# Decay attention and two MLPs in one kernel: seven instead of eight inner blocks of the first MLP beside attention, and three smaller moves

## The chip, the cores and the metric

The kernel runs on one core of one Trainium2 chip. The metric is the device time of one execution in microseconds (us). Three runs of the kernel before gave 1080.03, 1080.71 and 1081.43 us; their median, 1080.71 us, is the time before.

## The reference

Attention over 4 batches of 8 heads with 576 positions and 64 columns per head, with a decay from a cumulated logarithm and a causal mask; then a leaky MLP over all 2304 tokens; then a gated MLP.

```python
B, H, S, D = 4, 8, 576, 64
scores = np.matmul(q, k.transpose(0, 1, 3, 2)) / np.sqrt(D)
cum = np.cumsum(np.log(np.clip(f, 0.0001, 1.0)), axis=-1)
scores = np.where(causal, -1e9, scores + cum[:, :, :, None] - cum[:, :, None, :])
attn = softmax(scores)                      # max taken off, 1e-9 added to the sum
x = (attn @ v).transpose(0, 2, 1, 3).reshape(2304, 512)
h = x @ w_in                                # 512 -> 2048
x = (np.maximum(h, 0) + alpha * np.minimum(h, 0)) @ w_out
out = ((x @ w_a) * (x @ w_b)) @ w_out2      # 512 -> 1536 -> 512
```

The weights come in double precision. Products are made in parts: a number is split into a first, rounded part and a rest, and three matmuls (first by first, first by rest, rest by first) stand for one.

## The kernel before

**Attention with a part of the first MLP.** 32 heads go one after the other through the list in `order(u)`: scores (tiles `sc`), softmax (`softmax_in`), two halves of the probabilities in fp16 (`p_hi`, `p_lo`), a DMA transpose, and the product with v (`pv`, two heads later). The v of a head is scaled and split into two fp16 parts by `split_v`, three operations on GpSimd (POOL) for 26 of the 32 heads. The first MLP's 16 inner blocks of 128 columns are cut into three groups: blocks 0 to `F1A`-1 are made beside attention, blocks to 11 in a first pass over all tokens afterwards, blocks 12 to 15 in a second pass (`PASSES`). What stands beside attention is `mlp1a`: for each half batch of 288 tokens, 12 matmuls for each block's hidden part (tiles `h`) and 12 for its share of the output (tiles `y`), so 24 matmuls of 288 columns for each block and half batch. A batch's MLP can begin once its 8 heads are done; `rates` says how much of it stands beside each head. `before_x` makes the program finish batch 0 before batch 2 takes its buffers.

**Weights.** Each weight block goes through `rounded` and `parts`: a DMA on SyncE's queue, an Abs on ScalarE (ACT, L138), three integer operations on VectorE (DVE, L140 to L142), a copy on ACT (L146) and a subtraction on POOL (L147). Beside attention there is one staging buffer; the list `ws` names the head at which each of the 16 weights (8 `in`, then 8 `out`) is issued.

**The two passes** go over the tokens in blocks of 384: 24 matmuls of 384 columns for each inner block (tiles `hb` and `ya`). The second pass ends with `pair_parts`: the second MLP is made with seven products in place of eight for a pair of token blocks, and wants sums and differences of the pair's quarters. `put` splits one such quarter sum (ACT copy L942, POOL subtraction L943) and writes it to DRAM through one of four `yhl` buffers.

**The second MLP** visits the three pairs of token blocks in three groups of inner blocks: 36 slots of seven products (tiles `p`, 6 matmuls of 384 columns each, from weights `w_a` and `w_h`), whose sums are multiplied in `both` into tiles `gg`, and then into the output (tiles `o`) one slot later or more, in `unit`. Weights `b` take four DVE subtractions and five tiles' worth of parts (tile `w_h`); `when` says at which slot the later weights are issued.

A scheduler with its own timeline reorders the instructions of each engine; every engine then executes its own row in order. So the order on an engine, not the code alone, says what stands behind what.

Of the kernel before, what the change touches and what calls it, by code (L numbers as in the profile page):

```python
# [13 lines left out]
AF = mybir.ActivationFunctionType  # L14
ALU = mybir.AluOpType
# [3 lines left out]
B, H, S, D = 4, 8, 576, 64  # L19
T = B * S  # L20
# [11 lines left out]
TB = 384  # L32
# [13 lines left out]
    psm=3,  # L46
    first=10,
    rates=[0, 1, 1, 1, 0.8, 1.15, 1.15, 0.95],
    ws=[0, 1, 2, 3, 4, 5, 6, 7, 8, 8, 9, 9, 10, 10, 11, 11],
    native=10,  # L50
    pre=1,
    we=0,
# [14 lines left out]


LAGM = 2
F1A = _P.get("f1a", 8)  # L70

F1B = 12
PASSES = (F1A, F1B), (F1B, NF1)
# [9 lines left out]
FG = 4  # L83
# [9 lines left out]
def decay_attention_then_two_mlps(ctx, tc, q, k, v, f, w_in, w_out, alpha, w_a, w_b, w_o, out):  # L93
    nc = tc.nc
    pe, dve, act, pool, sp = nc.tensor, nc.vector, nc.scalar, nc.gpsimd, nc.sync

    left, mid, right = ExitStack(), ExitStack(), ExitStack()
    def lpool(stack, name, bufs, side="left", **kw):
        return stack.enter_context(tc.tile_pool(name=name, bufs=bufs, side=side, reuse_waits="tile", **kw))
# [49 lines left out]
    def weight(kind, i, p, after=None):  # L149

        x = rounded(kind, i, after)
        if kind == "b":

            xa = ap_["xa"]
            s = mp["stage"].tile([128, 8, 128], F32, tag="ws", name=f"ws_{i}", bufs=1)
            t = W["h", i] = p.tile([128, 2, 10, 128], F32R, tag="h", name=f"w_h{i}")
            dve.tensor_tensor(s[:, 0:2], x[:, 0:2], xa[:, 0:2], op=ALU.subtract)
            dve.tensor_tensor(s[:, 2:4], x[:, 2:4], s[:, 0:2], op=ALU.subtract)
            dve.tensor_tensor(s[:, 4:6], x[:, 2:4], x[:, 0:2], op=ALU.subtract)
            dve.tensor_tensor(s[:, 6:8], xa[:, 2:4], s[:, 2:4], op=ALU.subtract)  # L160
# [163 lines left out]
    def split_v(n):  # L324

        if whole(n):
            return
        vs = ap_["vs", n % 3]
        t = halves(n)
        scale = ap_["vm", (n // H) % 2][:, 1:2]  # L330
        pool.tensor_scalar(vs[:, :, 2], vs[:, :, 1], scale, 1.0, op0=ALU.mult, op1=ALU.mult)
        pool.tensor_scalar(t[:, :, 0:D], vs[:, :, 2], 1.0, 0.0, op0=ALU.mult, op1=ALU.add)
        pool.tensor_tensor(t[:, :, D:], vs[:, :, 2], t[:, :, 0:D], op=ALU.subtract)

    def halves(n):
# [456 lines left out]
    if True:  # L792
        w1 = lpool(left, "w1", 2 * F1A)
# [103 lines left out]
        yp = lpool(pctx, "passes", 4)  # L897
        todo = [(kind, i, w1) for i in range(F1B, NF1) for kind in ("in", "out")]
        todo += [(kind, i, hp[0] if kind == "b" else w1) for i in range(2) for kind in "abo"]
        todo += [("o", 2, w1), ("a", 2, w1)]  # L900
        bl = list(blocks())
        runs = [(p, t0, n) for p in range(2) for t0, n in bl]
        due = 0.0
# [27 lines left out]
                    continue  # L931
                pair_parts(t0 // TB, e, ya)

        kept = {}

        def pair_parts(blk, e, ya):

            pair, odd = divmod(blk, 2)

            def put(x, j, c):  # L940
                yh = yp.tile([128, 2, TB], F32R, tag="yhl", name=f"yhl_{pair}_{j}_{c}")
                act.copy(yh[:, 0], x)  # L942
                pool.tensor_tensor(yh[:, 1], x, f32(yh[:, 0]), op=ALU.subtract)  # L943
                sp.dma_start(f32(yq_d)[:, pair, j, c::2], f32(yh))

            if not odd:
                kept[e] = ya[e]
                put(ya[e], 0 if e < 2 else 3, e % 2)
            elif e >= 2:
                c = e - 2  # L950
                a11, a12, a21, a22 = kept[c], kept[e], ya[c], ya[e]
                s1 = yp.tile([128, TB], F32, tag="s1", name=f"s1_{pair}_{c}", bufs=2)
                dve.tensor_tensor(s1, a21, a22, op=ALU.add)
                put(s1, 2, c)
                dve.tensor_tensor(a21, a11, a21, op=ALU.subtract)
                put(a21, 5, c)
                dve.tensor_tensor(a11, s1, a11, op=ALU.subtract)
                put(a11, 1, c)
                put(a22, 6, c)
                dve.tensor_tensor(a12, a12, a11, op=ALU.subtract)  # L960
                put(a12, 4, c)

        Y = []
        visits = [0, 1, 2, 1, 0, 1, 2]
# [12 lines left out]
        for ri, (p, t0, n) in enumerate(runs):  # L977
            f0, f1 = PASSES[p]
            xh, xl = cur
            if ri + 1 < len(runs):  # L980
                cur = load_pair(xh_d, xl_d, *runs[ri + 1][1:], f"x{runs[ri + 1][0]}")
            st = {}
            for fi in range(f0, f1):
                w = W["in", fi]
                hps = pst.tile([128, 512], F32, tag="mm", name=f"hb_{t0}_{fi}")
                for c in range(C):
                    mm3(hps[:, :n], w[:, 0, c], w[:, 1, c], xh[:, c, :n], xl[:, c, :n], c == 0, c == C - 1)
                g = gp_.tile([128, 2, TB], F32R, tag="g", name=f"gb_{t0}_{fi}")
                leaky(hps, n, fi, tp, g[:, 0, :n], g[:, 1, :n])
                later(partial(passes_out, p, t0, n, fi, g, st))  # L990
                due += 0.4
                while len(todo) > 0 and due >= 1 and (ri, fi) > (0, f0 + 1):
                    due -= 1
                    weight(*todo.pop(0), ap_["last"])
                if p and t0 == 0 and fi == f0 + LAGM - 1:
                    w2ctx.close()
                    mp["yq"] = lpool(right, "yq", 4, "right")
                    ga_ = lpool(right, "ga", 3, "right")
                if p and t0 in (3 * TB, 5 * TB) and fi == f0:
                    for _ in range(4 if t0 == 3 * TB else 2):  # L1000
                        load_y()
        load_y()
        while todo:
            weight(*todo.pop(0), ap_["last"])
        while behind:
            behind.pop(0)()
        load_y()
        pctx.close()
        hp.append(lpool(left, "h2", FG // 2))
        op_ = lpool(left, "os", 3)  # L1010


        turns = [(g_, pair) for g_ in range(NG) for pair in range(NPAIR)[::(1, -1)[g_ % 2]]]
        slots = [(i, fi) for i in range(len(turns)) for fi in range(FG)]
        when = {0: [("b", 2), ("a", 3)], 1: [("b", 3), ("o", 3)]}
        for g_ in range(1, NG):
            s_ = (g_ * NPAIR - 1) * FG
            for fi in range(FG):
# [125 lines left out]
```

## Time and profile before

| what | value |
| --- | --- |
| median of three runs | 1080.71 us |
| profiled execution, its own time | 1082.8 us |
| its span, first to last instruction | 1081.0 us |
| TensorE busy (matmul) | 1011.7 us, 94% |
| VectorE busy | 717.5 us, 66% |
| ScalarE busy | 502.9 us, 47% |
| GpSimd busy | 560.4 us, 52% |
| granted clock of TensorE, mean | 0.976 |

Times in rows are us from the span's start. A matmul's duration overlaps that of the next, so the distance from one start to the next is what it costs in a dense row. PE is TensorE, PEld its weight loads. The shares are means over stages with different limits; what a change is worth is read stage by stage.

### The profile page before, as it was taken

To read this page: it belongs to the slowest core of one execution; us is meant where nothing else is said; L and a number is where in the kernel's file an instruction comes from. 1 tells how busy PE (TensorE), PEld (TensorE's weight loads), DVE (VectorE), ACT (ScalarE), POOL (GpSimd) and SP (SyncE) were. 2 spreads that over 40 slices of the span, in tenths; PEclk is the share of its full clock that TensorE was granted. 3 is DMA by queue.
4 is the path that set the end of the run, shared out by engine and by line. 5 is a ranking of instruction groups with operands and counts; after the bars stand their busy time and mean duration, and the time that the engine had idled before them with its cause. 6 is when DMAs were issued, how large, how long until landed. Compare 5 with 4: busy or idle time off the path is not lost.

```text
span 1081.0 us, 18236 instructions
## 1 busy us (share of the span) xinstructions
PE 1011.7 (94%) x6207; PEld 942.6 (87%) x6207; DVE 717.5 (66%) x1504; ACT 502.9 (47%) x1222; POOL 560.4 (52%) x662
## 2 busy tenths in 40 slices
PE   5989766999999999999999996899999999999998
PEld 3667655999899999999999995899989999899997
DVE  6688899558878836253457666655986558974553
ACT  6878866668778744333343533322433113321110
POOL 4366998747879845343346857522444224541111
PEclk9989977999999999999999998899999999999999
DMA  5776967757697495476767997636327383454623
GB/s 147 182 179 194 197 142 146 157 163 138 124 206 149 91 276 173 157 236 234 233 230 260 354 377 254 241 116 253 107 88 271 138 306 123 130 189 159 243 88 108
DMA packets 235969, 204.24 MB, mean 189 GB/s; under 512 B 152228, under 2 KB 209060, under 8 KB 235876
## 3 DMA queue, kind: packets, MB, share of 16 engines
q1 hardware_dynamic: 231268, 198.36, 62.0%
q10 hardware_dynamic: 4608, 4.72, 1.3%
q8 instruction: 49, 0.80, 0.3%
q14 instruction: 44, 0.36, 0.1%
HBM read 131.55 MB, written 50.17 MB: 168 GB/s over the span
## 4 chain that ended last, share of the span: by engine, by line
PE 55%; DVE 8%; POOL 4%; issue 3%; ACT 2%; DMA 1%; POOLq 0%; DVEq 0%; ACTq 0%
PE p L736 7%; PE p L738 7%; PE p L737 7%; PE o L738 4%; PE o L737 4%; PE o L736 4%; PE ya L737 3%; PE hb L738 3%; PE hb L736 3%; PE hb L737 3%; PE ya L738 3%; PE ya L736 3%; PE y L737 1%; PE y L738 1%; PE y L736 1%
## 5 line engine op out<-in xcount | busy, mean ns | idle before, releaser
L736 PE MATMUL p<-yq,w_h 128*128 128x384 f32 x360 | 122.6, 341 | 7.9 <-ACT w_h L146 6.4
L737 PE MATMUL p<-yq,w_h 128*128 128x384 f32 x360 | 122.0, 339 | 0.0
L738 PE MATMUL p<-yq,w_h 128*128 128x384 f32 x360 | 121.4, 338 | 0.0
L1077 POOL TENSOR_TENSOR gg<-tc,gg 128x384 fp32r<-128x384 f32 x36 | 37.0, 1027 | 113.5 <-ACT gg L1076 103.2
L736 PE MATMUL o<-w_o,gg 128*128 128x512 f32 x216 | 84.8, 394 | 4.1 <-ACT gg L1076 4.1
L1077 POOL TENSOR_TENSOR gg<-td,gg 128x384 fp32r<-128x384 f32 x36 | 37.3, 1036 | 93.7 <-ACT gg L1076 87.9
L737 PE MATMUL o<-w_o,gg 128*128 128x512 f32 x216 | 85.1, 394 | 0.0
L738 PE MATMUL o<-w_o,gg 128*128 128x512 f32 x216 | 84.4, 395 | 0.0
L736 PE MATMUL y<-g,w_out 128*128 128x288 f32 x256 | 78.0, 310 | 6.1 <-ACT w_out L146 4.2
L733 POOL TENSOR_TENSOR gb<-lt,gb 128x384 fp32r<-128x384 f32 x48 | 50.0, 1042 | 62.5 <-ACT gb L732 62.5
L736 PE MATMUL h<-xh,w_in 128*128 128x288 f32 x256 | 77.4, 305 | 3.7 <-DVE lt L731 3.4
L736 PEld LDWEIGHTS p<-yq,w_h 128*128 128x128 f32 x360 | 68.1, 189 | 12.4 <-ACT w_h L146 6.9
L737 PE MATMUL y<-g,w_out 128*128 128x288 f32 x256 | 76.9, 303 | 1.9 <-POOL g L733 1.9
L428 ACT ACTIVATE s<-s,nm 128x512 f32<-128x512 f32 (+3 forms) x128 | 71.4, 559 | 11.2 <-DVE nm L427 10.5
L1076 ACT CAST gg<-tc 128x384 fp32r<-128x384 f32 x36 | 18.5, 514 | 123.4 <-DVE tc L1075 122.9
L737 PE MATMUL h<-xl,w_in 128*128 128x288 f32 x256 | 75.7, 296 | 0.0
L738 PE MATMUL h<-xh,w_in 128*128 128x288 f32 x256 | 75.2, 294 | 0.0
L731 DVE SCALAR_TENSOR_TENSOR lt<-lu,nal,hb 128x384 f32<-128x384 f32 x48 | 29.3, 611 | 68.3 <-ACT lu L730 66.7
L738 PE MATMUL y<-g,w_out 128*128 128x288 f32 x256 | 74.2, 300 | 0.1
L737 PEld LDWEIGHTS p<-yq,w_h 128*128 128x128 f32 x360 | 68.1, 189 | 3.5
L427 DVE CUSTOM_DVE_ANT_0 s<-sc,maskz 128x512 f32<-128x512 f32 (+3 forms) x128 | 60.2, 485 | 12.9 <-PE sc L415 6.9
L738 PEld LDWEIGHTS p<-yq,w_h 128*128 128x128 f32 x360 | 67.8, 188 | 0.2
(217 smaller groups left out, 3307.2 us busy)
## 6 DMA issues: line engine op xcount, KB each, us to landing
yq<-yq_d SPq DMA_DIRECT2D x49, 768.0 KB
yq_d<-yhl SPq DMA_DIRECT2D x42, 384.0 KB
yl<-ya_d SPq DMA_DIRECT2D x48, 192.0 KB
po_d<-os SPq DMA_DIRECT2D x36, 256.0 KB
os<-po_d SPq DMA_DIRECT2D x36, 256.0 KB
wr_in<-in_moe_w_in SPq DMA_DIRECT2D x16, 512.0 KB
wr_out<-in_moe_w_out SPq DMA_DIRECT2D x16, 512.0 KB
wr_a<-in_moe_w_a SPq DMA_DIRECT2D x12, 512.0 KB
```

The source lines that it names most:

```text
L427: dve.tensor_tensor_reduce(s, o, m, -0.125, 3.0e38, ALU.add, ALU.min, nm)
L428: act.activation(s, s, AF.Exp, bias=nm, scale=-1.0, accum_out=sm)
L731: dve.scalar_tensor_tensor(t, u, nal[:, fi:fi + 1], hp[:, :n], op0=ALU.mult, op1=ALU.add)
L733: pool.tensor_tensor(gl, t, f32(gh), op=ALU.subtract)
L736: pe.matmul(o, lh, rh, start=start, stop=False)
L737: pe.matmul(o, lh, rl, start=False, stop=False)
L738: pe.matmul(o, ll, rh, start=False, stop=stop)
L1076: ap_["last"] = act.copy(g[:, 0], o).ins
L1077: pool.tensor_tensor(g[:, 1], o, f32(g[:, 0]), op=ALU.subtract)
```

## The change

Four edits. `F1A` is 7 and not 8: one block fewer beside attention for each half batch, one more (block 7) in the first pass, two of the `w1` weight buffers moved to the first pass's pool, and a list `ws` of 14 weights. In `split_v` the first fp16 part is made on ACT from the loaded v, with the scale, and no longer on POOL from the scaled v. The third `b` weight of the second MLP is issued during the passes into a pool of its own, and not at the second MLP's slot 0. And for the last pair of token blocks the sums of `pair_parts` are put off: ten steps, of which one is issued after each of the first ten products of the second MLP.

```diff
-    ws=[0, 1, 2, 3, 4, 5, 6, 7, 8, 8, 9, 9, 10, 10, 11, 11],
+    ws=[0, 1, 2, 3, 4, 5, 6, 7, 7, 8, 8, 9, 9, 10],
-F1A = _P.get("f1a", 8)
+F1A = _P.get("f1a", 7)
         pool.tensor_scalar(vs[:, :, 2], vs[:, :, 1], scale, 1.0, op0=ALU.mult, op1=ALU.mult)
-        pool.tensor_scalar(t[:, :, 0:D], vs[:, :, 2], 1.0, 0.0, op0=ALU.mult, op1=ALU.add)
+        act.activation(t[:, :, 0:D], vs[:, :, 1], AF.Copy, scale=scale)
         pool.tensor_tensor(t[:, :, D:], vs[:, :, 2], t[:, :, 0:D], op=ALU.subtract)
...
-        todo += [("o", 2, w1), ("a", 2, w1)]
+        todo += [("o", 2, w1), ("a", 2, w1), ("b", 2, hp)]
...
+            def less(o, x, y, j, c):
+                dve.tensor_tensor(o, x, y, op=ALU.subtract)
+                put(o, j, c)
...
-                put(s1, 2, c)
-                dve.tensor_tensor(a21, a11, a21, op=ALU.subtract)
-                put(a21, 5, c)
-                dve.tensor_tensor(a11, s1, a11, op=ALU.subtract)
-                put(a11, 1, c)
-                put(a22, 6, c)
-                dve.tensor_tensor(a12, a12, a11, op=ALU.subtract)
-                put(a12, 4, c)
+                steps = [
+                    partial(put, s1, 2, c),
+                    partial(put, a22, 6, c),
+                    partial(less, a21, a11, a21, 5, c),
+                    partial(less, a11, s1, a11, 1, c),
+                    partial(less, a12, a12, a11, 4, c),
+                ]
+                if blk == T // TB - 1:
+                    put_off.extend(steps)
+                    return
+                for step in steps:
+                    step()
...
                     ga_ = lpool(right, "ga", 3, "right")
+                    hp.append(lpool(right, "h2", FG // 2, "right"))
...
-        while todo:
-            weight(*todo.pop(0), ap_["last"])
+        assert not todo
...
-        when = {0: [("b", 2), ("a", 3)], 1: [("b", 3), ("o", 3)]}
+        when = {0: [("a", 3)], 1: [("b", 3), ("o", 3)]}
...
                 if leaves:
                     load_y()
+                if put_off:
+                    put_off.pop(0)()
                 return o
```

What the scheduler makes of it is seen in the order of the engines. First TensorE at heads 16 and 17. `sc_16` and `sc_17` are scores of these heads, `y_0_0` the output of batch 0's first half batch, `w_out7` and `w_out6` the last weight that it needs before and now, `tqk_17` a transpose for head 17. Before:

```order
L414 MATMUL sc_17_3_2570<-U1_1_156,T1_1_155 128x512
L415 MATMUL sc_17_3_2570<-TU2_1_157 128x512
L414 MATMUL sc_17_1_2597<-U1_1_156,T1_1_155 128x256
L415 MATMUL sc_17_1_2597<-TU2_1_157 128x256
L738 MATMUL y_0_0_0_1611<-g_0_0_1233,w_out7_1593 128x288
L738 MATMUL y_0_0_1_1697<-g_0_0_1233,w_out7_1593 128x288
L738 MATMUL y_0_0_2_1768<-g_0_0_1233,w_out7_1593 128x288
L414 MATMUL sc_17_0_2605<-U1_1_156,T1_1_155 128x128
L415 MATMUL sc_17_0_2605<-TU2_1_157 128x128
```

Now:

```order
L738 MATMUL y_0_0_0_1572<-g_0_0_1243,w_out6_1383 128x288
L738 MATMUL y_0_0_1_1655<-g_0_0_1243,w_out6_1383 128x288
L738 MATMUL y_0_0_2_1723<-g_0_0_1243,w_out6_1383 128x288
L380 MATMUL tqk_17_0_2263<-ident_90,qkn_17_2114 128x96 x3
L380 MATMUL tqk_17_1_2273<-ident_90,qkn_17_2114 128x96 x3
L414 MATMUL sc_16_2_2291<-U1_0_147,T1_0_146 128x384
L414 MATMUL sc_16_0_2312<-U1_0_147,T1_0_146 128x128
L415 MATMUL sc_16_2_2291<-TU2_0_148 128x384
L415 MATMUL sc_16_0_2312<-TU2_0_148 128x128
```

The last matmuls of `y_0_0` stood among head 17's scores and now stand ahead of head 16's; the rest of batch 0 follows them directly in both orders. Counted over the whole order, the `h` and `y` matmuls in TensorE's row are, before and now: ahead of head 16's first score 150 and 147, from head 16's first score to head 18's 240 and 195, from there to head 31's 630 and 552, and behind it 516 and 450; in all 1536 and 1344.

Second, GpSimd where the first MLP ends and the second begins. `yhl_2_*` are the last pair's parts (`put`), `gg_s_b` the products of slot s (block b of the pair), `w_h2` and `w_h3` the third and fourth `b` weight. Before:

```order
L1077 TENSOR_TENSOR gg_1_0_8342<-tc_1_8281,gg_1_0_8342 128x384
L943 TENSOR_TENSOR yhl_2_5_0_8128<-yl_1_1920_0_8072,yhl_2_5_0_8128 128x384
L943 TENSOR_TENSOR yhl_2_1_0_8133<-yl_1_1536_0_7908,yhl_2_1_0_8133 128x384
L943 TENSOR_TENSOR yhl_2_6_0_8137<-yl_1_1920_2_8090,yhl_2_6_0_8137 128x384
L1077 TENSOR_TENSOR gg_1_1_8385<-td_1_8282,gg_1_1_8385 128x384
L943 TENSOR_TENSOR yhl_2_4_0_8142<-yl_1_1536_2_7944,yhl_2_4_0_8142 128x384
L943 TENSOR_TENSOR yhl_2_2_1_8149<-s1_2_1_8147,yhl_2_2_1_8149 128x384
L943 TENSOR_TENSOR yhl_2_5_1_8154<-yl_1_1920_1_8074,yhl_2_5_1_8154 128x384
L943 TENSOR_TENSOR yhl_2_1_1_8159<-yl_1_1536_1_7910,yhl_2_1_1_8159 128x384
L943 TENSOR_TENSOR yhl_2_6_1_8163<-yl_1_1920_3_8092,yhl_2_6_1_8163 128x384
L943 TENSOR_TENSOR yhl_2_4_1_8168<-yl_1_1536_3_7946,yhl_2_4_1_8168 128x384
L147 TENSOR_TENSOR w_h2_8225<-wx_b2_8219,w_h2_8225 128x256
```

Now:

```order
L1087 TENSOR_TENSOR gg_0_1_8200<-td_0_8097,gg_0_1_8200 128x384
L943 TENSOR_TENSOR yhl_2_2_0_8105<-s1_2_0_8087,yhl_2_2_0_8105 128x384
L943 TENSOR_TENSOR yhl_2_6_0_8117<-yl_1_1920_2_8056,yhl_2_6_0_8117 128x384
L943 TENSOR_TENSOR yhl_2_5_0_8130<-yl_1_1920_0_8038,yhl_2_5_0_8130 128x384
L943 TENSOR_TENSOR yhl_2_1_0_8143<-yl_1_1536_0_7874,yhl_2_1_0_8143 128x384
L943 TENSOR_TENSOR yhl_2_4_0_8166<-yl_1_1536_2_7910,yhl_2_4_0_8166 128x384
L147 TENSOR_TENSOR w_h3_8263<-wx_b3_8257,w_h3_8263 128x256
L943 TENSOR_TENSOR yhl_2_2_1_8182<-s1_2_1_8090,yhl_2_2_1_8182 128x384
L943 TENSOR_TENSOR yhl_2_6_1_8195<-yl_1_1920_3_8058,yhl_2_6_1_8195 128x384
L1087 TENSOR_TENSOR gg_1_0_8282<-tc_1_8206,gg_1_0_8282 128x384
L147 TENSOR_TENSOR w_h3_8263<-ws_3_8262,w_h3_8263 128x512
L943 TENSOR_TENSOR yhl_2_5_1_8216<-yl_1_1920_1_8040,yhl_2_5_1_8216 128x384
```

The third `b` weight stood behind all ten of the last pair's parts and is now far ahead of them, in the passes; seven parts now stand between slot 0's second product and slot 1's first, where three of them stood between slot 1's two products before.

## Rows read from the trace of the kernel before

**Rows 1.** Windows: length; busy us (count) of PE, PEld, DVE, ACT, POOL; PE clock; DMA.
```profile
101.80:173.20 71.40, 52.76 (x385) 45.33 (x383) 66.27 (x171) 55.53 (x154) 64.75 (x81) 0.88 0.79 175
173.20:190.90 17.70, 11.18 (x61) 9.11 (x60) 14.22 (x37) 10.01 (x29) 12.68 (x18) 0.69 0.78 142
190.90:225.90 35.00, 35.00 (x264) 34.35 (x263) 14.78 (x32) 18.24 (x48) 20.19 (x29) 0.96 0.73 190
225.90:365.70 139.80, 136.70 (x1153) 130.76 (x1152) 113.88 (x318) 112.93 (x324) 110.83 (x168) 1.00 0.68 142
365.70:442.90 77.20, 75.36 (x593) 73.94 (x593) 39.48 (x73) 37.23 (x90) 42.14 (x46) 1.00 0.64 184
442.90:664.00 221.10, 220.78 (x1261) 219.67 (x1260) 127.41 (x201) 87.78 (x177) 117.62 (x106) 1.00 0.79 269
664.00:682.00 18.00, 7.53 (x22) 5.95 (x21) 7.97 (x11) 6.55 (x15) 13.13 (x13) 0.62 0.56 201
```

**Rows 2.** Timeline of GpSimd, the last two `w_out` weights beside attention.
```profile
173.67 1.76 POOL L147 TENSOR_TENSOR w_out<-wx_out,w_out 128x512 fp32r<-128x512 f32 x1 [0.45 <-ACT w_out L146]
...
188.78 1.28 POOL L147 TENSOR_TENSOR w_out<-wx_out,w_out 128x512 fp32r<-128x512 f32 x1
```

**Rows 3.** Timeline of TensorE, batch 0's outputs around 190 us.
```profile
188.44 0.61 PE L736 MATMUL y<-g,w_out 128*128 128x288 f32 x1 [1.85 <-ACT w_out L146]
...
189.08 0.44 PE L736 MATMUL y<-g,w_out 128*128 128x288 f32 x1
189.32 0.44 PE L737 MATMUL y<-g,w_out 128*128 128x288 f32 x1
...
194.27 0.29 PE L738 MATMUL y<-g,w_out 128*128 128x288 f32 x1
194.40 0.29 PE L736 MATMUL y<-g,w_out 128*128 128x288 f32 x1
```

**Rows 4.** Groups by line and shape, GpSimd and VectorE, 101.8 to 173.2 us.
```profile
L332 POOL TENSOR_SCALAR vs<-vs 128x320 f16<-128x320 f32 x6 | 3.7, 623 | 0.2
...
L142 DVE SCALAR_TENSOR_TENSOR wx_out<-wr_out,wx_out 128x512 int32<-128x512 int32 x7 | 6.7, 956 | 0.1
```

**Rows 5.** The same groups, ScalarE and GpSimd, 225.9 to 365.7 us.
```profile
L486 ACT ACTIVATE p_hi<-s,ri 128x384 f16<-128x384 f32 x13 | 8.0, 614 | 1.6 <-DVE ri L451 1.1 <-issue 0.2
...
L622 ACT ACTIVATE x<-pv,vm 64x256 f32<-64x256 f32 x13 | 6.1, 469 | 0.7 <-PE pv L597 0.3
...
L332 POOL TENSOR_SCALAR vs<-vs 128x320 f16<-128x320 f32 x12 | 5.5, 459 | 0.5
```

**Rows 6.** Timeline of VectorE and of GpSimd, 660 to 665 us.
```profile
660.38 1.37 DVE L955 TENSOR_TENSOR yl<-yl,yl 128x384 f32<-128x384 f32 x1
...
664.36 0.54 DVE L955 TENSOR_TENSOR yl<-yl,yl 128x384 f32<-128x384 f32 x1
...
660.19 1.14 POOL L943 TENSOR_TENSOR yhl<-s,yhl 128x384 fp32r<-128x384 f32 x1 [1.65 <-ACT yhl L942]
```

**Rows 7.** Timeline of TensorE where the second MLP begins.
```profile
668.84 0.80 PE L736 MATMUL o<-w_o,gg 128*128 128x512 f32 x1 [4.09 <-ACT gg L1076]
...
677.10 0.69 PE L736 MATMUL p<-yq,w_h 128*128 128x384 f32 x1 [6.38 <-ACT w_h L146]
...
678.55 0.52 PE L736 MATMUL p<-yq,w_a 128*128 128x384 f32 x1
678.87 0.52 PE L737 MATMUL p<-yq,w_a 128*128 128x384 f32 x1
...
685.00 0.41 PE L736 MATMUL p<-yq,w_h 128*128 128x384 f32 x1 [1.24 <-DVE td L1093]
...
685.60 0.33 PE L736 MATMUL p<-yq,w_h 128*128 128x384 f32 x1
685.77 0.34 PE L737 MATMUL p<-yq,w_h 128*128 128x384 f32 x1
```

**Rows 8.** Timeline of ScalarE at the same place.
```profile
673.41 0.51 ACT L942 CAST yhl<-yl 128x384 fp32r<-128x384 f32 x1 [2.97 <-DMA yq_d<-yhl]
```

More of the change, by code (lines that the diff above doesn't have):

```diff
@@ L932, in passes_out @@
                 pair_parts(t0 // TB, e, ya)
-        kept = {}
+        kept, put_off = {}, []
         def pair_parts(blk, e, ya):
@@ L993, in decay_attention_then_two_mlps @@
                     due -= 1
-                    weight(*todo.pop(0), ap_["last"])
+                    kind, i, pl = todo.pop(0)
+                    weight(kind, i, pl[1] if pl is hp else pl, ap_["last"])
                 if p and t0 == 0 and fi == f0 + LAGM - 1:
@@ L1002, in decay_attention_then_two_mlps @@
         load_y()
-        while todo:
-            weight(*todo.pop(0), ap_["last"])
+        assert not todo
         while behind:
@@ L1007, in decay_attention_then_two_mlps @@
         load_y()
-        pctx.close()
-        hp.append(lpool(left, "h2", FG // 2))
-        op_ = lpool(left, "os", 3)
         turns = [(g_, pair) for g_ in range(NG) for pair in range(NPAIR)[::(1, -1)[g_ % 2]]]
         slots = [(i, fi) for i in range(len(turns)) for fi in range(FG)]
-        when = {0: [("b", 2), ("a", 3)], 1: [("b", 3), ("o", 3)]}
+        when = {0: [("a", 3)], 1: [("b", 3), ("o", 3)]}
         for g_ in range(1, NG):
@@ L1061, in decay_attention_then_two_mlps @@
         for s_, (i, fi) in enumerate(slots):
+            if s_ == FG - 2:
+                assert not put_off
+                pctx.close()
+                op_ = lpool(left, "os", 3)
             g_, pair = turns[i]
```

## The prediction

> **What bounds the kernel now.** I read the windows view by stage first, then the counts in the engines' orders, then timelines at the places where a stage's busiest engine stands still. Stage bounds are the starts of heads' first score matmuls, counted off in TensorE's timeline (head 10 at 101.8 us, 16 at 173.2, 17 at 190.9, 18 at 225.9, 31 at 365.7); batch 3's MLP ends at 442.9, the passes at 664.
>
> [Rows 1] show four different limits. Heads 10 to 15: TensorE is busy 52.8 of 71.4 us, VectorE 66.3 (93%) and GpSimd 64.8 (91%); the two small engines bind, at a granted clock of 0.88. Head 16, 17.7 us: nothing is full, TensorE 11.2 at clock 0.69. What it waits for is batch 0's first output, which needs every `w_out` weight: the last two are split at 173.7 and 188.8 [rows 2], and TensorE's `y` rows wait for them [rows 3]. From 190.9 to 225.9 TensorE is full (35.0 of 35.0): batch 0 must be finished before later heads may go on. Heads 18 to 30: TensorE 136.7 of 139.8 (98%), VectorE, ScalarE and GpSimd 79 to 81%; TensorE binds. Up to 664 it stays full. At 664 to 682 it works 7.5 of 18 us, at clock 0.62, and [rows 7] name the three stalls: 4.09 us for a `gg`, 6.38 us for `w_h` and 1.24 us for a sum.
>
> **The change part by part.** Prices are against the profiled execution, 1082.8 us, 2.1 above the median of the three runs; I take 2.1 off at the end.
>
> *One inner block moves.* In a dense row a 288-column matmul costs 0.13 us (194.27 to 194.40 in [rows 3]), a 384-column one 0.173 (685.60 to 685.77 in [rows 7]). Removed beside attention: 24 matmuls x 8 half batches = 192. Added to the first pass: 24 x 6 token blocks = 144, and the passes are full of matmuls (220.8 of 221.1 us, [rows 1]), so they cost all of 144 x 0.173 = **+24.9 us**. For TensorE alone that is an exchange (192 x 0.13 = 25.0); what counts is how much of the 25 us the attention stages give back, and how much idle time goes with it.
>
> - Head 31 and batch 3: 66 fewer matmuls (516 to 450 in the order) where TensorE is busy 75.4 of 77.2 us: 66 x 0.13 = **-8.6**. Two weights more (10, not 8) are made here; VectorE, ScalarE and GpSimd are at 48 to 55%, which hides them. If that cover failed the passes would wait for one staging chain.
> - Heads 18 to 30: 78 fewer matmuls, 78 x 0.13 = 10.1 us if TensorE goes on binding, nothing if another engine takes over. ScalarE's 112.9 us get 13 more activations of 320 columns (between 0.469 for 256 and 0.614 for 384, [rows 5], so about 0.54 each, +7.0) and lose some three leaky blocks, about 2.5; 117 us in 130 would be 90%. VectorE's 113.9 less 2 in 130 is 86%. VectorE has been 93% full in heads 10 to 15, so such fills are possible, with more waiting. I take **-7**, two thirds, as VectorE and ScalarE both stay under the fullest row seen; ends -10.1 and 0.
> - Heads 16 and 17 (52.7 us): the order carries 195 matmuls, not 240, and the last `w_out` block now stands one head earlier, ahead of `sc_16`. Upper bound of the gain: TensorE's own work at full clock is 11.2 x 0.69 + 35.0 x 0.96 = 41.3, less 45 x 0.13 = 5.9, that is 35.4 and a gain of 17.3. Lower bound: only the 45 matmuls go and the wait for weights stays, 5.9. I take **-11**, near the middle: the chain is one block shorter, and its last two blocks came 15.1 us apart [rows 2], more than head 16's 6.5 us of idle; the rest is the clock's.
> - Heads 10 to 15 have the same five weights and the same matmuls within 3. GpSimd loses six operations of 0.623 us, 3.7 us [rows 4], ScalarE, 78% full, gains six of 0.54. VectorE is as full as GpSimd, so I take **-2**; ends -4 and +1.
> - Heads 0 to 9 have one weight fewer, whose dearest VectorE operation is 0.956 us [rows 4]; no engine is full there. **-1**; ends -3 and +1.
>
> *v's first part.* Priced above: POOL work away, ACT work added, beside others in both. The last subtraction now waits for ScalarE as well as for GpSimd; queued behind it on GpSimd are the next head's probabilities, and two heads of lag lie before `pv` needs the result.
>
> *The start of the second MLP.* Now: after 664 the ten parts of the last pair stand on ScalarE and GpSimd ahead of `w_h2`, and one of them waits 2.97 us for a buffer whose write to DRAM is under way [rows 8]; the products of slot 2 stand behind `w_h2`. The change takes `w_h2` out and puts it into the passes, where ScalarE is 40% and GpSimd 53% busy. The three stalls are 11.7 us; 16 matmuls from 677.1 to 682 then go at 0.32 us apart, not 0.173 [rows 7], 2.3 us. So up to 14.0 us are to be had. What is late next: `gg_1_0`, which seven parts and a piece of `w_h3` now precede on GpSimd. At 1.14 us each [rows 6] these eight and `gg_1_0` itself take 10.3 us, from `gg_0_1` on, which comes about 2 us behind its last product (a sum, a copy, a subtraction); TensorE has 72 matmuls in between in its order, at least 72 x 0.173 = 12.5 us. That just fits. One buffer wait like the 2.97 us one would show through, so I take 14 - 3 = **-11**; ends -14 and, with four such waits, -2. Their ten DMAs stand ahead of the loads of pair 1's quarters on SyncE's queue; those are wanted only three slots later. VectorE's six subtractions move too, 0.54 to 1.37 us each [rows 6], 3 to 8 us over two slots; if it has no room for them, the sums of slot 1 are late and `gg_1_0` with them.
>
> Sum: 24.9 - 8.6 - 7 - 11 - 2 - 1 - 11 = -15.7; 1082.8 - 15.7 - 2.1 = **1065 us**.
>
> *A rule against the row.* A VectorE subtraction of two tiles in SBUF took 1.37 us while GpSimd worked on 384 columns and 0.54 us while it did not get in the way [rows 6]. So busy time on VectorE is in part time spent waiting for GpSimd, and an operation taken from GpSimd may free both. The Trainium skill (SBUF — State Buffer, Who interferes with whom) says that a VectorE instruction with two SBUF inputs and a GpSimd one that reads SBUF exclude each other for the whole instruction; the trace agrees in kind. It is a rival below, since my terms give VectorE nothing for it.
>
> **The rivals.**
>
> *Lock:* each POOL operation removed frees VectorE by as much. Then heads 10 to 15 give 3.7 and heads 18 to 30, with VectorE at about 106 us, keep TensorE full and give 10.1: 1.7 + 3.1 = 4.8 better, **1060**. For it: rows 6. Against: not every POOL operation meets a two-input one.
>
> *Another engine takes over in heads 18 to 30:* ScalarE at 90% with its waits for VectorE; 7 us lost, **1072**. For it: all three small engines are at 80% already. Against: each has 26 to 29 us of idle there.
>
> *The stall moves:* the put-off parts, in one queue with `gg`, stall slots 1 and 2. With four buffers' waits the gain is 2, **1074**. For it: the parts fit with hardly anything to spare. Against: before, ten of them in a row met one such wait of 2.97 us.
>
> *No earlier weights:* heads 16 and 17 give 5.9 only, **1070**. Against: the order.
>
> *Slower:* the clock falls in heads 18 to 30. It is 1.00 (2.4 GHz) where TensorE idles 2%, 0.88 at 26% and 0.69 at 37% [rows 1], and a 288-column matmul then goes 0.24 us apart (1.2 GHz; 189.08 to 189.32, [rows 3]), 0.11 dearer. Half of the 552 matmuls there at the low level cost 30 us, and the 7 us are lost: **1102**. It decides from about 100 matmuls at the low level on, (15.7 - 7 + 2.2) / 0.11. Against it: by my terms TensorE is still 95% busy there.
>
> **How the numbers follow.** Forecast 0.45, lock 0.17, another engine 0.13, stall moves 0.13, no earlier weights 0.07, clock 0.05. The forecast's own ends, added as independent (3, 2, 5, 3, 3), give 7 or 8 either way; so 1058 to 1072 for it alone; the rivals but the last lie at 1060 to 1074, and the lock's lower end at 1053. So 1053 to 1076. A measurement of this kernel tells 0.2%, 2.2 us, from no change. Faster needs a time under 1078.5: all cases but the clock, and but two misses together (another engine and the stall, 1081). So faster 0.92, same 0.03, slower 0.05.
>
> **What would show it.** The stretch from head 18's to head 31's scores about 133 us and TensorE at 95% in it; heads 16 and 17 together near 42 us and no `y` row waiting for `w_out` there; batch 3's MLP over about 45 us; the passes about 246 us and full; between the last `ya` and slot 3 at most 3 us of idle, and a clock of 1.00. It is wrong if heads 18 to 30 keep 140 us, if `gg` rows wait several us in slots 1 to 3, or if the passes are not full and so cost more than 24.9.

## The result and the profile after

Four runs of the changed kernel gave 1065.49, 1067.18, 1069.42 and 1072.90 us, a median of **1068.3 us**; the kernel before had a median of 1081.06 us beside them. The ratio is **0.9888, 95% [0.9851, 0.9925]**: faster, inside the range, 3 us above the forecast. The profiled execution took 1067.18 us with a span of 1065.4: 15.6 us less than the profiled one of before, where the sum of my terms said 15.7. That the sum is so exact is chance, as the stages show.

Windows of the changed kernel by stage, columns as in [rows 1]. The bounds are those of [rows 1], with two differences: heads 16 and 17 are one row, and the passes end here at the last `ya`, not at 664 as in [rows 1], where the last `ya` of the kernel before starts at 652.9:

```profile
99.50:170.80 71.30, 53.24 (x381) 45.84 (x380) 67.49 (x173) 58.44 (x161) 61.05 (x76) 0.88 0.80 178
170.80:204.70 33.90, 33.90 (x277) 33.22 (x276) 21.10 (x58) 24.34 (x67) 20.00 (x32) 1.00 0.72 150
204.70:342.10 137.40, 128.83 (x1075) 121.65 (x1074) 110.20 (x319) 115.33 (x335) 110.28 (x163) 0.99 0.79 166
342.10:409.90 67.80, 66.34 (x526) 65.21 (x526) 38.21 (x70) 34.30 (x84) 40.06 (x41) 1.00 0.68 195
409.90:641.90 232.00, 230.09 (x1317) 228.95 (x1316) 120.95 (x189) 92.81 (x188) 119.82 (x111) 1.00 0.74 251
641.90:671.30 29.40, 25.12 (x132) 22.84 (x131) 28.24 (x40) 10.97 (x23) 21.97 (x19) 1.00 0.57 204
```

Head 16's low clock (0.69) is gone: heads 16 and 17 are full at 1.00. Heads 18 to 30 are hardly shorter, and TensorE idles 8.6 us in them, where it idled 3.1. Laid side by side by the same instructions (first score matmuls of heads; last `ya` of the first pass; last `ya_1_1536` of the second; the first `p` of slots 3, 5 and 35), in us:

| stretch | before | after | difference | my term |
| --- | --- | --- | --- | --- |
| heads 0 to 9 | 101.8 | 99.5 | -2.3 | -1 |
| heads 10 to 15 | 71.4 | 71.3 | -0.1 | -2 |
| heads 16 and 17 | 52.7 | 33.9 | **-18.8** | -11 |
| heads 18 to 30 | 139.8 | 137.3 | **-2.5** | -7 |
| head 31 and batch 3 | 77.1 | 67.8 | -9.3 | -8.6 |
| first pass | 104.9 | 131.2 | +26.3 | +24.9 |
| second pass, most of it | 84.0 | 85.1 | +1.2 | 0 |
| to slot 3 of the second MLP | 55.6 | 45.2 | -10.4 | -11 |
| slots 3 and 4 | 23.3 | 24.4 | +1.1 | 0 |
| slots 5 to 34 | 343.7 | 343.2 | -0.5 | 0 |

Heads 0 to 9 need a warning. In twelve traces of this study, all but experiment 8's, they took between 99.5 and 103.9 us. Experiments 3 and 4 have the same order of instructions there, on every engine, as the changed kernel, and took 101.9 and 101.4 us where it took 99.5; so a difference of 2 us there tells nothing.

The last two `w_out` weights on GpSimd, which answer to [rows 2]:

```profile
158.16 1.70 POOL L147 TENSOR_TENSOR w_out<-wx_out,w_out 128x512 fp32r<-128x512 f32 x1
166.75 1.28 POOL L147 TENSOR_TENSOR w_out<-wx_out,w_out 128x512 fp32r<-128x512 f32 x1
```

They come 15.5 and 22.0 us earlier. TensorE, where the second MLP begins, which answers to [rows 7]:

```profile
656.89 0.44 PE L736 MATMUL p<-yq,w_a 128*128 128x384 f32 x1 [0.70 <-DVE lt L1105]
658.76 0.45 PE L736 MATMUL p<-yq,w_h 128*128 128x384 f32 x1 [0.55 <-DVE tc L1105]
662.80 0.50 PE L736 MATMUL o<-w_o,gg 128*128 128x512 f32 x1 [1.68 <-ACT gg L1086]
669.67 0.44 PE L736 MATMUL p<-yq,w_h 128*128 128x384 f32 x1 [1.34 <-DVE lu L1105]
```

Four waits of 4.3 us in all stand where three of 11.7 stood; the 6.38 us for `w_h` has gone, the one for `gg` is 1.68 and not 4.09, and the clock stays at 1.00. Over the whole stretch to slot 3, TensorE idles 7.4 us less (4.3 of 45.2 us, 11.7 of 55.6 before), and its 223 matmuls are busy 40.9 us where 224 took 43.9 at a clock of 0.88: 3.0 us of the 10.4 go with the higher clock.

### The profile page after: what moved, and what is told of

The parts are those of the page before. It is cut to its first block, busy times and chain, and to the rows that moved or that the text cites. A ratio compares the mean times of both kernels' runs of the same rounds, so it can differ in the third digit from the quotient of the medians.

```text
span 1065.4 us, 18161 instructions
## 1 busy us (share of the span) xinstructions
PE 1006.0 (94%) x6159; PEld 938.4 (88%) x6159; DVE 711.7 (67%) x1502; ACT 510.2 (48%) x1244; POOL 548.5 (51%) x634
## 4 chain that ended last, share of the span: by engine, by line
PE 65%; DVE 12%; ACT 7%; DMA 5%; POOL 5%; issue 4%; SPq 1%; ACTq 0%; POOLq 0%; DVEq 0%
PE p L736 7%; PE p L738 7%; PE p L737 7%; PE o L738 4%; PE o L736 4%; PE o L737 4%; PE ya L736 3%; PE ya L737 3%; PE ya L738 3%; PE hb L738 3%; PE hb L737 3%; PE hb L736 3%; PE h L736 2%; PE h L737 1%; PE h L738 1%
## 5 line engine op out<-in xcount | busy, mean ns | idle before, releaser
L733 POOL TENSOR_TENSOR gb<-lt,gb 128x384 fp32r<-128x384 f32 x54 | 55.9, 1035 | 59.0 <-ACT gb L732 58.3
L428 ACT ACTIVATE s<-s,nm 128x512 f32<-128x512 f32 (+3 forms) x128 | 71.3, 558 | 7.4 <-DVE nm L427 6.3
L736 PE MATMUL ya<-gb,w_out 128*128 128x384 f32 x216 | 71.1, 337 | 1.9 <-DVE yl L928 1.2
L737 PE MATMUL ya<-gb,w_out 128*128 128x384 f32 x216 | 72.7, 337 | 0.0
L738 PE MATMUL ya<-gb,w_out 128*128 128x384 f32 x216 | 72.5, 336 | 0.0
L731 DVE SCALAR_TENSOR_TENSOR lt<-lu,nal,hb 128x384 f32<-128x384 f32 x54 | 33.0, 611 | 57.9 <-ACT lu L730 52.1
L736 PE MATMUL h<-xh,w_in 128*128 128x288 f32 x224 | 67.3, 305 | 4.5 <-DVE lt L731 3.1
L427 DVE CUSTOM_DVE_ANT_0 s<-sc,maskz 128x512 f32<-128x512 f32 (+3 forms) x128 | 59.6, 484 | 15.2 <-PE sc L411 10.1
L736 PE MATMUL y<-g,w_out 128*128 128x288 f32 x224 | 66.6, 306 | 3.3 <-DVE lt L731 1.9
L737 PE MATMUL y<-g,w_out 128*128 128x288 f32 x224 | 66.7, 302 | 0.5 <-POOL g L733 0.5
```

The costliest lines, as they stand in the source:

```text
L427: dve.tensor_tensor_reduce(s, o, m, -0.125, 3.0e38, ALU.add, ALU.min, nm)
L428: act.activation(s, s, AF.Exp, bias=nm, scale=-1.0, accum_out=sm)
L731: dve.scalar_tensor_tensor(t, u, nal[:, fi:fi + 1], hp[:, :n], op0=ALU.mult, op1=ALU.add)
L733: pool.tensor_tensor(gl, t, f32(gh), op=ALU.subtract)
L736: pe.matmul(o, lh, rh, start=start, stop=False)
L737: pe.matmul(o, lh, rl, start=False, stop=False)
```

## The experiments

In each, "changed" is the kernel after, and times are medians. Stage times are of the profiled execution.

**1. v's first part back on GpSimd** (`e1_v_pool`), the other three edits kept.

```diff
-        act.activation(t[:, :, 0:D], vs[:, :, 1], AF.Copy, scale=scale)
+        pool.tensor_scalar(t[:, :, 0:D], vs[:, :, 2], 1.0, 0.0, op0=ALU.mult, op1=ALU.add)
```

> The changed kernel, but v's first fp16 part is made on GpSimd again; the other three edits stay. Theory A (v's edit costs more than it gives: in heads 18 to 30 ScalarE stands 5.5 us before this activation waiting for the load of v): heads 18 to 30 take 132 to 135 us, not 137.4, heads 16 and 17 stay at 34 us, total 1063 to 1067. Theory B (taking work off GpSimd is what shortens heads 10 to 17): heads 10 to 17 take 4 to 8 us longer, total 1071 to 1076.

Measured: 1062.22 us, ratio 0.9849 [0.9832, 0.9867]. Its windows for heads 10 to 15, 16 and 17, and 18 to 30:

```profile
99.50:180.50 81.00, 67.84 (x488) 62.38 (x487) 68.84 (x183) 61.11 (x172) 72.32 (x92) 0.85 0.78 176
180.50:200.30 19.80, 19.80 (x175) 19.24 (x173) 14.28 (x44) 15.88 (x46) 12.96 (x22) 1.00 0.86 166
200.30:335.90 135.60, 128.18 (x1070) 120.81 (x1068) 112.67 (x318) 111.07 (x321) 114.28 (x173) 1.00 0.78 168
```

Heads 10 to 17 take 100.8 us and not 105.2, heads 18 to 30 135.6 and not 137.4. (How the 100.8 divide between the first two rows is only a matter of which of batch 0's matmuls stand ahead of head 16's scores: 488 against 381 here.) The move of v's first part to ScalarE is not worth the 2 us that I gave it; it costs. Theory A has the sign, but not the place: it put the whole loss into heads 18 to 30, and more of it stands in heads 10 to 17.

**2. The block alone** (`e2_seven_alone`): the kernel before with `F1A` = 7 and its list of weights, nothing else.

```diff
-    ws=[0, 1, 2, 3, 4, 5, 6, 7, 8, 8, 9, 9, 10, 10, 11, 11],
+    ws=[0, 1, 2, 3, 4, 5, 6, 7, 7, 8, 8, 9, 9, 10],
...
-F1A = _P.get("f1a", 8)
+F1A = _P.get("f1a", 7)
```

> The kernel before with seven inner blocks and the list of 14 weights alone; v's first part, the third b weight and the last pair's sums as before. Theory A (the early last w_out block alone makes heads 16 and 17 short, the block costs 25 to 27 us in the passes, the start of the second MLP keeps its stall): attention about 33 us shorter, total 1072 to 1077. Theory B (without the relief of GpSimd attention gives back only the removed matmuls): attention 24 us shorter or less, total 1081 or more.

Measured: 1069.64 us, 0.9912 [0.9895, 0.9929]. Heads 10 to 30 take 235.3 us, 28.6 less than the 263.9 of before, the first pass 130.9. The stretch to slot 3 takes 53.4 us, 2.2 less than before and 8.2 more than the changed kernel's; TensorE in it:

```profile
658.26 0.79 PE L736 MATMUL o<-w_o,gg 128*128 128x512 f32 x1 [3.93 <-ACT gg L1076]
664.92 0.44 PE L736 MATMUL p<-yq,w_h 128*128 128x384 f32 x1 [1.12 <-ACT w_h L146]
672.84 0.41 PE L736 MATMUL p<-yq,w_h 128*128 128x384 f32 x1 [3.49 <-DVE td L1093]
```

The stalls of [rows 7] are there with other lengths. So the block's move, with its list of weights, gives all of the attention stages' gain by itself, and 2.2 us at the start of the second MLP with no edit there. Which of the two, fewer matmuls or a shorter chain of weights, gives how much was not run apart. Theory A came in kind, with a total 2 us under its range.

**3. The sums not put off** (`e3_sums_back`): changed, but the last pair's ten parts are issued at once, as those of the others.

```diff
-                if blk == T // TB - 1:
+                if blk == T // TB:
```

> The changed kernel, but the last pair's sums are not put off; the third b weight stays early. If the gg stall is the sums' alone: 4 to 6 us of idle come back at the start of the second MLP, total 1072 to 1075. If the sums are all of the 10.4 us that were gained there: 1078. If the early b weight is all of it: 1068.

Measured: 1067.12 us, 0.9889 [0.9874, 0.9904]; the stretch to slot 3 takes the same 45.21 us, and the same four waits stand in it (0.71, 0.56, 1.66 and 1.36 us). In GpSimd's order the parts, `gg` and `w_h` rows of the first slots stand alike with this edit and without it: the scheduler had already moved the parts behind the products. With the third `b` weight early, putting the sums off changes nothing.

**4. The weight late** (`e4_b2_late`): changed, but the third `b` weight is issued at slot 0 again, the sums put off.

```diff
-        todo += [("o", 2, w1), ("a", 2, w1), ("b", 2, hp)]
+        todo += [("o", 2, w1), ("a", 2, w1)]
...
-        when = {0: [("a", 3)], 1: [("b", 3), ("o", 3)]}
+        when = {0: [("b", 2), ("a", 3)], 1: [("b", 3), ("o", 3)]}
```

> The changed kernel, but the third b weight is issued at the second MLP's slot 0 again (into the pool on the right); the sums stay put off. If the w_h stall of 6.4 us was this weight standing behind the sums, and it now stands among them: 3 to 7 us of idle come back before slot 2, total 1071 to 1075. If the sums alone made the stall: 1068. If both edits only work together: 1078.

Measured: 1066.69 us, 0.9891 [0.9874, 0.9907]. TensorE's waits in the same place:

```profile
653.22 0.44 PE L736 MATMUL p<-yq,w_h 128*128 128x384 f32 x1 [0.90 <-DVE lu L1105]
...
657.32 0.69 PE L736 MATMUL p<-yq,w_a 128*128 128x384 f32 x1 [2.55 <-DVE lt L1105]
```

No wait for `w_h`, although the weight is issued at slot 0: with the ten parts out of its way it is in time. The stretch takes 46.4 us, 1.2 more than the changed kernel's, but the second pass takes 83.4, 1.7 less. The early weight's parts stand on VectorE in the passes, and there these two waits of the changed kernel are, which this one lacks:

```profile
596.17 0.41 PE L736 MATMUL ya<-gb,w_out 128*128 128x384 f32 x1 [0.79 <-DVE yl L928]
...
598.89 0.45 PE L736 MATMUL ya<-gb,w_out 128*128 128x384 f32 x1 [0.40 <-DVE yl L928]
```

So either of the two edits is enough, and both together give no more than one. What they give is less than the 10.4 us of the table, though: experiment 2, with neither, already has 53.4 us there and not 55.6. Against it putting off alone gives 7.0 us (46.4), and the early weight alone 8.2 (45.2), of which it gives back 1.7 in the second pass.

**5. Four buffers for v** (`e8_four_v`): changed, with four `vs` buffers and each v loaded one head earlier.

```diff
-        vs = ap_["vs", n % 3]
+        vs = ap_["vs", n % 4]
...
-                        load_v(u + 3 - LAG)
+                        load_v(u + 4 - LAG)
```

> The changed kernel with four buffers for v, not three, and each v loaded one head earlier; ScalarE still makes v's first fp16 part. Theory A1 (v's edit costs because ScalarE, in order, waits for the load of v): the waits of this activation go from about 8 us to under 2, and the total is 3 to 5 us below the changed kernel's 0.9888 of before, so about 0.985. Theory A2 (it costs because ScalarE's added work pushes the chain of w_out weights, with its one staging buffer, behind more heads): in this kernel's order the last w_out stands one head later still, so heads 10 to 17 get longer by 3 to 8 us although the load waits are gone, ratio 0.989 to 0.995.

Measured: 1071.21 us, 0.9908 [0.9889, 0.9928]. The test failed in its means: ScalarE waited 9.7 us for v's loads at L332 (heads 10 to 30), not less than the changed kernel's 7.9, and part of batch 0's MLP moved behind head 18's scores (heads 18 to 30 took 152.9 us, heads 10 to 17 94.4). It does not tell whether an early load would save the edit.

**6. v's edit alone** (`e9_v_alone`), in the kernel before.

```diff
-        pool.tensor_scalar(t[:, :, 0:D], vs[:, :, 2], 1.0, 0.0, op0=ALU.mult, op1=ALU.add)
+        act.activation(t[:, :, 0:D], vs[:, :, 1], AF.Copy, scale=scale)
```

> The kernel before with v's first fp16 part on ScalarE and nothing else changed. Theory A2: the last w_out weight stands behind head 16 and not ahead of it, heads 10 to 19 become 4 to 8 us longer, ratio 1.003 to 1.008. Theory B (relief of GpSimd, and of VectorE with it): heads 10 to 15 become 2 to 4 us shorter, ratio 0.996 to 0.999.

Measured: 1086.97 us, **1.0061 [1.0040, 1.0082]**: slower. Heads 10 to 30 take 268.0 us, 4.1 more. The last two weights on GpSimd are 11.0 and 9.6 us later than in [rows 2]:

```profile
184.65 1.69 POOL L147 TENSOR_TENSOR w_out<-wx_out,w_out 128x512 fp32r<-128x512 f32 x1
198.41 1.28 POOL L147 TENSOR_TENSOR w_out<-wx_out,w_out 128x512 fp32r<-128x512 f32 x1
```

In GpSimd's order the last one stands behind one head's probabilities more (16's) than before. The ratio is in theory A2's range; the relief of theory B did not come.

**7. Two of the four edits** (`e10_two_edits`): the block, its list and the put-off sums; v's first part on GpSimd and the third `b` weight at slot 0, as before. Its diff from the changed kernel is that of experiments 1 and 4 together.

> The changed kernel with v's first part on GpSimd again and the third b weight at the second MLP's slot 0 again, so that seven blocks and the put-off sums alone are left of the change. If the early b weight costs more in the second pass (1.7 us where the second pass waits for loads) than it gives at the start of the second MLP once the sums are put off: 1 to 2 us below the run without v's edit, ratio 0.983 to 0.984. If it gives more: 0.986.

Measured: **1061.93 us, 0.9822 [0.9808, 0.9837]**: the lowest ratio here, just under the range expected. It is clear of the changed kernel and of experiment 4; its interval overlaps that of experiment 1 (0.9849 [0.9832, 0.9867]). First pass 131.3, second 83.4, to slot 3 46.1 us.

**8. Two staging buffers for the weights** (`e13_two_stages`), in the kernel of experiment 7.

```diff
-        mp["stage"] = lpool(mid, "wstage", 1)
+        mp["stage"] = lpool(mid, "wstage", 2)
```

> The kernel of the run before in this call with two staging buffers for the weights beside attention, not one. Theory A2 (the chain of weights through one staging buffer sets when batch 0's MLP can run, and TensorE idles for it in heads 10 to 15): the last w_out is done by 110 to 120 us, not 157 to 189, TensorE's idle time in heads 10 to 15 falls from 13 to under 6 us and the clock there rises above 0.95, total 6 to 12 us less, ratio 0.973 to 0.978. Theory C (heads 10 to 15 are bound by VectorE and GpSimd whatever the weights do): the same work comes earlier but the heads take longer, total within 2 us of the run without the second buffer, ratio 0.982 to 0.986.

Measured: 1069.32 us, 0.9889 [0.9867, 0.9912]. The last `w_out` is split at 124.2 us and not 160.0. Windows of heads 0 to 9, 10 to 15, 16 and 17, 18 to 30:

```profile
0.00:107.90 107.90, 81.49 (x454) 61.93 (x455) 78.54 (x227) 83.60 (x212) 61.55 (x94) 0.95 0.73 188
107.90:178.70 70.80, 64.86 (x510) 60.58 (x510) 60.22 (x167) 56.16 (x164) 62.02 (x88) 0.93 0.73 156
178.70:197.90 19.20, 18.80 (x165) 18.05 (x164) 15.61 (x47) 14.47 (x43) 14.27 (x23) 1.00 0.82 165
197.90:342.80 144.90, 130.94 (x1054) 123.33 (x1055) 113.75 (x321) 112.95 (x323) 114.40 (x173) 0.95 0.78 161
```

Against experiment 7 (102.6, 79.6, 19.7, 136.0) what heads 10 to 17 win is lost in heads 18 to 30: the sum is 234.9 against 235.3, and heads 0 to 9, which now do the weights' work, take 5.3 more. Weights that come still earlier buy nothing: by theory A2 the ratio would be at most 0.978, by theory C at most 0.986, and the kernel is slower than both say.

**9 and 10. v's first part on ScalarE for half of the heads**: for heads 0 to 15 (`e6_v_mixed`), and for heads from 16 on (`e14_v_late`).

```diff
+        if n < 16:
             act.activation(t[:, :, 0:D], vs[:, :, 1], AF.Copy, scale=scale)
+        else:
+            pool.tensor_scalar(t[:, :, 0:D], vs[:, :, 2], 1.0, 0.0, op0=ALU.mult, op1=ALU.add)
```

> The changed kernel, but v's first fp16 part is made on ScalarE only for heads 0 to 15 and on GpSimd, as in the kernel before, from head 16 on. With ScalarE for all heads the profiled run took 4.4 us more in heads 10 to 17 and 1.7 us more in heads 18 to 30 than with GpSimd for all. Theory A (v's edit costs by putting the last w_out weight behind one more head's probabilities on GpSimd): the order of the weights is that of the changed kernel, so the last w_out is split at 165 to 168 us, heads 10 to 17 take about 105 us, heads 18 to 30 about 135.6; time about 1066.5 us, ratio 0.987 to 0.989. Theory B (it costs by ScalarE's activations waiting for v's load, wherever they stand, 5.5 of the 7.9 us of such waits being in heads 18 to 30): heads 10 to 17 stay near 105, but the larger part of the loss goes, about 1063.5 us, ratio 0.983 to 0.985.

> The opposite: the changed kernel with v's first fp16 part on GpSimd for heads 0 to 15, and on ScalarE only from head 16 on. Theory A (the weight chain): the last w_out is split near 157 us as with GpSimd for all heads, heads 10 to 17 take about 101 us, heads 18 to 30 about 137; time about 1063.5 us, ratio 0.983 to 0.985. Theory B (waits for v's load in heads 18 to 30): those waits of some 5 us stay, and with them the larger part of the loss; about 1066.5 us, ratio 0.987 to 0.989.

Measured: 1069.56 us, 0.9918 [0.9897, 0.9939], and 1066.58 us, 0.9888 [0.9864, 0.9911]. The last `w_out` on GpSimd in experiments 1, 9 and 10:

```profile
156.74 1.28 POOL L147 TENSOR_TENSOR w_out<-wx_out,w_out 128x512 fp32r<-128x512 f32 x1
167.60 1.28 POOL L147 TENSOR_TENSOR w_out<-wx_out,w_out 128x512 fp32r<-128x512 f32 x1
159.16 1.28 POOL L147 TENSOR_TENSOR w_out<-wx_out,w_out 128x512 fp32r<-128x512 f32 x1
```

By stage:

| v's first part on ScalarE for | last `w_out`, us | heads 0 to 9 | heads 10 to 17 | heads 18 to 30 |
| --- | --- | --- | --- | --- |
| all heads (changed) | 166.75 | 99.5 | 105.2 | 137.3 |
| no head (1) | 156.74 | 99.5 | 100.8 | 135.6 |
| heads 0 to 15 (9) | 167.60 | 101.4 | 105.1 | 136.2 |
| heads 16 on (10) | 159.16 | 102.2 | 100.7 | 137.5 |

The places in heads 10 to 17 are as theory A had them: they lose 4.4 us when the early heads' v is on ScalarE, and with it the last weight comes 7.6 to 10.9 us later. The totals fit neither theory. Both are 3.1 us above theory A's numbers. Theory B's number came for experiment 10 (1066.58 against 1066.5), but by it experiment 9 would be the faster of the two, and it measured 6 us above B's 1063.5. Nor do the halves add up: v's edit in all heads costs 0.4% (experiments 3 and 4 against 1), the late half alone as much (0.9888 against 0.9849), the early half 0.7%. The trace of experiment 10 is 4.8 us longer than that of experiment 1: 1.8 stand in heads 10 to 30, 1.0 in head 31 and batch 3, and 2.7 in heads 0 to 9, where traces differ without an edit; the later stages are 0.7 shorter.

The pair bears on the rival "lock" as well. Heads 18 to 30 of experiment 10, whose counterpart with v on GpSimd is the third row of experiment 1:

```profile
202.90:340.40 137.50, 128.37 (x1066) 120.67 (x1065) 112.96 (x319) 117.67 (x336) 108.77 (x162) 1.00 0.81 167
```

GpSimd is busy 5.5 us less and ScalarE 6.6 more; VectorE 112.96 us for 319 instructions against 112.67 for 318. It got nothing by the operations taken from GpSimd. In the changed kernel, it is true, VectorE is busy only 110.20 us for 319 there; but in experiment 9, where v's first part is on GpSimd in these heads, it is 110.96 us for 316. The relief goes with the order that the early heads leave behind, and it shortened neither stretch.

**11. Six blocks** (`e12_six`), in the kernel of experiment 7, with twelve weights in the list.

```diff
-    ws=[0, 1, 2, 3, 4, 5, 6, 7, 7, 8, 8, 9, 9, 10],
+    ws=[0, 1, 2, 3, 4, 5, 6, 6, 7, 7, 8, 8],
...
-F1A = _P.get("f1a", 7)
+F1A = _P.get("f1a", 6)
```

> The version with two of the four edits (block move and put-off sums, 1061.9 us), but six inner blocks beside attention and twelve weights listed there. One more block costs the first pass 26 us, as measured for the first one moved. Theory S (heads 10 to 30 are now bound by VectorE and GpSimd, not by TensorE): the heads give back 9 us in head 31 and batch 3, about 2 in heads 0 to 9 and at most 8 in heads 10 to 30; about 1069 us, ratio 0.987 to 0.991. Theory T (TensorE still binds in the heads): heads 10 to 30 lose the 126 matmuls of the block at 0.13 us, 16.4 us; about 1061 us, ratio 0.980 to 0.984.

Measured: 1077.65 us, 0.9982 [0.9965, 0.9999]. Near theory S in kind, 9 us beyond its number. Heads 10 to 30 give back 6.9 us (228.4), but head 31 with batch 3 and the first pass cost 22.4 more, not 17. Windows of head 31 with batch 3, and of the first pass's first token block:

```profile
330.10:391.50 61.40, 51.85 (x387) 49.67 (x385) 34.84 (x66) 29.16 (x70) 35.58 (x40) 0.89 0.73 213
391.50:425.50 34.00, 31.03 (x169) 30.96 (x169) 23.35 (x30) 15.77 (x33) 19.97 (x15) 0.95 0.73 234
```

and TensorE's greatest wait in the first of these, in total, times and longest:

```profile
PE pv L596 <- DMA PT_lo<-p_lo: 7.6, 2, 4.7
```

In the changed kernel the stretch of the first row is 66.34 of 67.80 us full. Here TensorE runs out of MLP work while the last heads' probabilities are transposed by DMA. Of six, seven and eight blocks, seven is the least with which the attention stages still had enough to do.

## Why the prediction came out right, and where it did not

The time is right because three large terms are, the passes, head 31 with batch 3 and the start of the second MLP, and because the misses in heads 10 to 30 nearly cancel (+1.9, -7.8 and +4.5 us by the table). That they cancel is luck. Of the signs that I named, full passes and the clock of 1.00 at the second MLP's start came. Heads 18 to 30 came at 137.4 us and 94% (133 and 95% named), heads 16 and 17 at 33.9 us (42), and 4.3 us of idle stand before slot 3 (3).

**The block's move.** Right in its sign and its main sizes. The passes pay 21.01 - 16.81 = 4.20 us for each token block from the second on (24 matmuls at 0.175), the first one 5.29, in all 26.3 against my 24.9. Head 31 and batch 3 gave 9.3 against 8.6. Heads 10 to 15 finish six weights in either trace, and not the five that I named; that changes no term.

**Heads 16 and 17: the mis-sized term.** I took -11, between "only the matmuls go" and "the wait for weights goes whole". It was -18.8, a little beyond the upper end of 17.3. The stretch is as full as TensorE can be (33.90 of 33.90 us) at clock 1.00: the wait went whole, and the low clock of head 16 with it. Short waits for `w_out` were left ahead of it. These are TensorE's waits in heads 10 to 17 of the changed kernel, in total, times and longest:

```profile
PE y L738 <- POOL w_out L147: 1.9, 3, 1.0
PE y L736 <- ACT w_out L146: 1.3, 1, 1.3
```

so "no `y` row waiting" was not quite met. The lower end rested on a wait that stays; the chain of weights moved by 22.0 us, more than the wait and head 16's idle time together. Experiment 2 shows that the block's move makes it: without v's edit heads 10 to 17 give even 24.6 us (124.1 to 99.5).

**Heads 18 to 30: the other one.** I took -7 of 10.1; it was -2.5. By the windows row TensorE's busy time fell by 7.9 us (136.70 to 128.83), and its idle time rose by 5.5. A small part is v's edit: 1.7 us by experiment 1, about 1 us over all traces. In experiments 1, 2 and 7, without that edit, the stretch takes 135.6 to 136.0 us, with it (the changed kernel, experiments 3 and 4) 136.4 to 137.4; so without it -4: TensorE is 128.2 us busy of 135.6 in experiment 1, 95%, with VectorE at 83%. In experiment 7 its waits there are ten kinds, none over 1.7 us in all, most of their time for VectorE. So of the rival "another engine takes over" a part came, by many small waits and not by a full engine. What heads 18 to 30 lack, heads 16 and 17 gave: my terms for heads 10 to 30 were -20, and -21.4 came.

**v's first part.** I called it hidden and worth about 2 us in heads 10 to 15. Alone it is a loss of 0.61% [0.40, 0.82] (experiment 6). Experiment 7, which is experiment 4 without it, is 0.7% faster, and kernels that keep it (experiments 3 and 4, 0.9889 and 0.9891) stand clear of experiment 1 (0.9849) in the same set of runs. That the edit costs is shown. The step that failed is "queued behind it on GpSimd are the next head's probabilities": what is queued there, too, is the chain of weights. In the orders the edit puts the last `w_out` behind one head's probabilities more in the kernel before, and behind two heads' more with seven blocks (18 `p_lo` rows of GpSimd stand ahead of it in the changed kernel, 14 in experiment 1, two to a head). Slip and loss in heads 10 to 17 come together in every kernel with seven blocks but those of experiments 5 and 8, which have other buffers: 103.4 to 105.2 us with the early heads' v on ScalarE (changed, 3, 4, 9), 99.3 to 100.8 without (1, 2, 7, 10). That the slip makes the loss is argued: no run held the weights in place and moved v, and in experiment 8 weights that came 36 us earlier gained nothing. In the heads after 16 ScalarE stands still for v's load, as the group of the changed kernel's heads 18 to 30 says (busy, mean ns of one, and idle time just before them):

```profile
L332 ACT ACTIVATE vs<-vs,vm 128x320 f16<-128x320 f32 x13 | 7.3, 561 | 5.5 <-DMA vs<-in_v 5.5
```

My price for the activation itself was right (0.56 us; 0.54 estimated); its wait, 5.5 us over 13 heads, was in no term. Whether that wait makes what these heads lose is not shown, since experiment 5 did not take it away.

**The lock.** It gave no time: experiment 6 took 26 operations from GpSimd and came out slower, and experiment 10 shows VectorE's busy time unmoved by those of heads 18 to 30. The rule that I weighed (the Trainium skill, SBUF — State Buffer, Who interferes with whom) may hold for a pair of instructions, as [rows 6] show one. VectorE's busy time does move by 2.5 us with the order (110.20 us in the changed kernel, 112.67 in experiment 1), but the stretch with less of it is the longer one.

**The start of the second MLP.** -10.4 against -11, and slots 3 and 4 gave 1.1 back. The size is right, in part by luck, and the cause was told wrong: I summed two edits where either alone does it, and 2.2 of the 10.4 us come with the block's move (experiment 2). The early weight also brought 1.2 us of waits into the second pass, which I had priced at nothing because VectorE, ScalarE and GpSimd have room there by their shares. The rival "the stall moves" came in small: from 640 to 675 us ScalarE met four waits for `yhl` buffers, 5.2 us in all, the longest 2.1, and TensorE waited 1.68 us for a `gg` in that stretch.

**Slower, by the clock.** It did not happen: 0.99 in heads 18 to 30, with TensorE idle 6% there. In experiment 8's heads 18 to 30 the clock did fall, to 0.95, with TensorE 10% idle.

What stays open: which wait makes the loss of v's edit, in heads 18 to 30 above all, and why the late half alone costs as much in all as the whole edit; how much of the block's gain is the shorter list of weights; and what sets heads 0 to 9 between 99.5 and 103.9 us. Whether the spread of the changed kernel's runs (1065.5 to 1072.9) comes from there is not known, as each kernel has one trace.

## What to carry to other kernels

Price an operation that changes its engine by what stands behind it in both queues: 26 small operations moved from the fuller engine to an emptier one cost 0.6%, and with the move a chain of weights slipped in GpSimd's order, which is the likely reason. When several edits aim at one stall, run each without the others: here either of two was enough, and the kernel with only two of the four edits has the lowest ratio (0.9822 [0.9808, 0.9837]). And moving work from a stage that waits to one that is full pays as long as the first stage keeps something to cover its longest wait: the block from eight to seven gave 0.9%, the next one took 1.6% back.

## What the runs showed of the hardware that I had not expected

The first ten heads, the same work in every kernel but for a weight or two, took between 99.5 and 103.9 us from trace to trace, and kernels with the very same order of instructions there differ by 2.4 us; so differences of under 4 us there are not read from single traces. And the granted clock does not follow from a stage's idle share alone: 1.00 with 5.5% idle (heads 18 to 30 of experiment 1), 0.96 with 5.6% (144.3 of 152.9 us busy, the same heads of experiment 5), 0.95 with 9.6% (experiment 8) and 0.89 with 15.6% (head 31 with batch 3 of experiment 11). What a wait costs beyond its own length is seen in [rows 7]: behind the one of 6.38 us matmuls start 0.32 us apart, and 0.173 later.
